# Interleaved quarters: the two transfers of each expert-weight tile take alternate pieces of the rows

## The chip, the cores and the metric

The kernel runs on one core of a Trainium2 chip. The core has a matrix engine (TensorE, PE in the profile, with its weight loads as PEld), a vector engine (VectorE, DVE), an activation engine (ScalarE, ACT), a general engine (GpSimd, POOL) and a small engine that here only issues transfers (SyncE, SP). Transfers are carried out by 16 DMA engines that all issuing engines share. Each engine works through its own list of instructions in order, and waits on semaphores where it needs the result of another engine or of a transfer.

The metric is the device time of one execution in microseconds (us), lower being better. The profile's clock covers the span from the first to the last instruction of the program; the time of the execution is a little longer.

## What is computed

Two blocks stand one after the other. The first is a linear attention with a delta rule, for 4 batches of 8 heads, 768 steps and a head size of 48:

```python
for t in range(S):
    kt, vt, bt = (k_n[:, :, t], v[:, :, t], beta[:, :, t, None])
    y[:, :, t] = np.einsum('bhd,bhde->bhe', q[:, :, t], state)
    v_old = np.einsum('bhde,bhd->bhe', state, kt)
    state = state + bt[:, :, :, None] * np.einsum('bhd,bhe->bhde', kt, vt - v_old)
```

`k_n` is `k` with each row scaled to length one. Its output, 3072 rows of 384 columns, goes into a mixture of 8 experts with 4 slots each. A softmax over the rows mixes them into 32 slots, each expert puts its 4 slots through two products, and a softmax over the slots mixes them back:

```python
logits = x @ phi
d = softmax over rows of logits;  c = softmax over slots of logits
slot_input = d.T @ x                      # 32 x 384
for e in range(E):                        # 8 experts, 4 slots each
    h = np.maximum(slot_input[e] @ w1[e], 0.0)   # w1[e]: 384 x 1024
    slot_out[e] = h @ w2[e]                      # w2[e]: 1024 x 384
return c @ slot_out
```

All inputs and the output are 32-bit floats. The weights `w1` and `w2` are 12.6 MB each (8 x 384 x 1024 x 4 bytes).

## The kernel before

**The sequence is cut into chunks.** The 768 steps are 12 chunks of 64. For a chunk, `load` (L399) brings `k` and `v`, and `load_q` (L416) `q`, in rows of 192 bytes; `prep` (L481) transposes them and multiplies keys with keys and queries. The recursion within a chunk becomes the inverse of a triangular matrix. `invert` (L550) works for two chunks at a time on blocks of 16, column by column, with small multiplications and subtractions (all issued through the helper `tt`, L277) that a table gives to DVE or to POOL. `join` (L641) puts blocks of 16 together into blocks of 64: `madd` (L702, also through L277) makes a sum that the products at L716 need. `step` (L803) then takes the chunks one after the other, since the state passes from each to the next; its products are at L782, L791, L821 and L840. `route` (L894) and `pair` (L910) gather the logits and the running softmax for the slots.

**The experts come last.** `first` (L1080) multiplies the slots with `w1` (L1090) for four experts at a time, in two halves of 512 columns; `qq` is the group of four. `prod` of the second stage (L1119, the product at L1123) multiplies with `w2`, in two passes `h` over 192 of the 384 output columns; each pass goes through all 32 tiles of `w2`. L1142 mixes the slots back to rows, L277's neighbours L281 and L283 copy results out of the accumulators, and L1150 writes the output.

**The weights are loaded long before.** A tile of `w1` is 128 partitions by 1024 columns (one of the 3 slices `kk` of an expert); there are 24. A tile of `w2` is 128 partitions by 768 columns (rows `2 tp` and `2 tp + 1` of each partition); there are 32. Each tile is brought by two transfers, issued one right after the other by the same engine, SP or POOL (the loops at L1021 and L1032). Tiles go into one memory in which each address is used many times over, so a transfer can start only when what stood there has been read.

**The order is fixed by hand.** Every piece of work is an `Op` with the engines that could do it. Three tables written into the file set everything: `ORDER` (L17) is the order of all pieces, and so the order on every engine; `ALTS` (L108) names the engine of each; `PLACE` (L75) its addresses. `Plan.run` (L186) issues the pieces in that order. The semaphores and waits are not written in the kernel: a layer below finds out which instructions touch the same memory and places them. A transfer adds to one of eight semaphores per kind of queue, taken in turn (one set for SP and ACT, one for POOL).

SP carries 32 transfers of `w1`, 46 of `w2` and most of `q`, `k` and `v`. POOL carries 16 of `w1`, 18 of `w2` and a few of the others, between its share of the arithmetic.

Of the kernel before, what the change touches and what calls it, by code (L numbers as in the profile page):

```python
# [196 lines left out]
def kernel(  # L197
# [17 lines left out]
    E, Dm, F = moe_w1.shape  # L215
# [14 lines left out]
    def A(b, n=None):  # L230
        if b.psum:
            return pb[:, b.addr:b.addr + b.size, :]
        return sb[:, b.addr:b.addr + (n or b.size)]
# [37 lines left out]
    def dq(a, b, c):  # L271
        return [("SP", a), ("POOL", b)] + ([("ACT", c)] if c else [])

    ENG = {"SP": nc.sync, "ACT": nc.scalar, "POOL": nc.gpsimd, "DVE": nc.vector}
# [104 lines left out]
    def perm():  # L379
        for x in H2:  # L380
# [3 lines left out]
          w=[(cmA, 1)])  # L384
# [14 lines left out]
    def load(src, n, pad):  # L399
        t = kslot[n % NK] if pad else pl.buf(KW)  # L400
        s = src.rearrange("b h s d -> s (b h) d")

        d = lambda: A(t).rearrange("p (x d) -> p x d", x=16)[:, :, 0:D]
        for r in H2:
            h0 = 16 * (1 - r)
            parts = [(64 * r, 64, slice(0, 16, 2), n * C, slice(h0, h0 + 16, 2))]
            for k in range(4):
                parts.append((64 * r + 16 * k, 16, slice(1, 16, 2), n * C + 48 - 16 * k, slice(h0 + 1, h0 + 16, 2)))

            def go(e, ps=parts):  # L410
                for p0, w, x, t0, hs in ps:
                    ENG[e].dma_start(out=d()[p0:p0 + w, x], in_=s[t0:t0 + w, hs])  # L412
            pl.op(dq(2.6, 2.95, 2.5 if src is k and n < 2 else None), None, go, w=[(t, 2 * r)], bus=1.5, nd=5)
        return t

    def load_q(n):  # L416
# [3 lines left out]
        for r in H2:  # L420
# [6 lines left out]
          w=[bnat], bus=0.1)  # L427
# [35 lines left out]
    def turn(src, n, a):  # L463
        if n not in KQ:
            KQ[n] = pl.buf(2048)
        dst = KQ[n]
        for h in H2:
            ps = pl.buf(1, psum=True)

            def go(h=h, ps=ps):  # L470
                for j in range(4):
                    x = P * (4 * h + j)
                    nc.tensor.transpose(A(ps)[:, 0, P * j:P * j + P], A(src)[:, x:x + P], ident())  # L473
            pl.op("PE", 0.53, go, r=[src, cident], w=[ps], rec=4, hold=[dst], act=512)

            def tev(e, h=h, ps=ps):
                copy(e, kqv(dst)[:, 4 * h:4 * h + 4, :, a],
                     A(ps)[:, 0].rearrange("p (j r t) -> p j r t", j=4, r=2))
            pl.op(ev(512), None, tev, r=[ps], w=[(dst, 2 * a + h)])
# [305 lines left out]
    def query(n):  # L785
        pY = late[n][0]

        def go():
            for j in range(8):
                for r in H2:  # L790
                    mm(A(pY)[ha(1 - r), j // 4, 96 * (j % 4):96 * (j % 4) + 96], kqv(KQ[n])[:, j, r, 1], Sv(n)[:, j, r],  # L791
                       start=j % 4 == 0)
        pl.op("PE", 1.47, go, r=[KQ[n], Sz[n % 2]], w=[pY], rec=32, act=1536)
# [227 lines left out]
    for e in range(E):  # L1021
        for kk in range(NKT):
            w1b[e, kk] = t = done.pop(0) if done else pl.buf(F)
            pl.tag = ("w1", e)

            def go(q, e=e, kk=kk, t=t):
                s = moe_w1[e].rearrange("(p k) f -> p k f", k=NKT)
                for x in H2:
                    ENG[q].dma_start(out=A(t)[:, 512 * x:512 * x + 512], in_=s[:, kk, 512 * x:512 * x + 512])
            pl.soft = [chain[8]]  # L1030
            pl.op(dq(0.8, 1.2, None), None, go, w=[t], bus=1.5, nd=2)
    for e in range(E):  # L1032
        for tp in range(NFC // 2):
            w2b[e, tp] = t = last.pop() if last and e == E - 1 else pl.buf(2 * Dm)
            pl.tag = ("w2", e)

            def go(q, e=e, tp=tp, t=t):
                s = moe_w2[e].rearrange("(p t) d -> p t d", t=NFC)
                for x in H2:
                    ENG[q].dma_start(out=A(t)[:, Dm * x:Dm * x + Dm], in_=s[:, 2 * tp + x])  # L1040
            pl.soft = [chain[N - 1]]
            pl.op(dq(0.8, 1.2, None), None, go, w=[t], bus=1.15, nd=2)
    pl.soft = []
# [138 lines left out]
```

## Time and profile before

| | us |
|---|---|
| three runs | 298.03, 295.66, 298.94; median 298.03 |
| the profiled execution | 296.42 |
| its span | 294.7 |
| PE busy in the span | 228.9 (78%) |
| DVE busy | 197.6 (67%) |
| ACT busy | 145.2 (49%) |
| POOL busy | 140.2 (48%) |
| granted PE clock, mean | 0.938 of full speed |

SP's transfers (queue q1) took 42.3% of what 16 DMA engines could do in the span, POOL's (q0) 15.0%.

How to read what is quoted. A row such as `187.01 3.30 POOL L1029 DMA_DIRECT2D sb<-in_moe_w_dram  x6 [2.04 <-ACT sb L513]` comes from the timeline: start and length in us, engine, line, operation, what it writes and reads, how many in a row, and in brackets the idle time of the engine before it and who ended it. `SPq` is the list of SP, where an issue stands with the time that it took SP to issue it, not with the transfer's own. `sb` is the on-chip memory, `pb` the accumulators, `in_moe_w_dram` the weights `w1` or `w2`: the line tells which. A row `POOLq DMA_DIRECT2D x16, 256.0 KB, 5.3` of the DMA view gives the number of issues, the size of each and the median time in us from issue to landing. A row of a line's own view (`L1040 SPq ... x46: 327/335/1575`) gives the shortest, median and longest duration in ns.

### The profile page before, as it was taken

The numbers are of one execution on the slowest core, as the hardware profiler recorded it, in microseconds if no ns is written. First come the engines' busy times: TensorE is split into PE (matmuls) and PEld (weight loads), VectorE is DVE, ScalarE is ACT, GpSimd is POOL, SyncE is SP. The second block draws the span as 40 slices with busy tenths as digits, with TensorE's granted clock in tenths as the row PEclk, the third lists the DMA queues.
The fourth block names the chain that finished last, engine by engine and source line by source line (L and its number), as shares of the span: only waits on it lengthen the run. The fifth ranks groups of instructions, "written<-read, shape, count | busy, mean of one in ns | idle before, by whom it ended". The sixth has DMA issues, their size and how long they took to land.

```text
span 294.7 us, 14440 instructions
## 1 busy us (share of the span) xinstructions
PE 228.9 (78%) x6252; PEld 186.2 (63%) x6252; DVE 197.6 (67%) x504; ACT 145.2 (49%) x325; POOL 140.2 (48%) x225
## 2 busy tenths in 40 slices
PE   0784778982988897798979877787866988999950
PEld 0663677872887786686868775766654864366640
DVE  3468979989866689777699889883773667213130
ACT  1253487774828466668736768562311532230321
POOL 8997569454493364226762545641640320200460
PEclk9997599999579999999899999999997999999985
DMA  8979642453431361336545407785696599990887
GB/s 147 162 155 166 111 79 56 97 107 56 87 56 34 73 118 33 62 54 136 116 94 118 153 4 232 215 190 177 200 349 218 178 349 375 349 364 13 213 226 206
DMA packets 81519, 45.13 MB, mean 153 GB/s; under 512 B 63520, under 2 KB 74704, under 8 KB 81456
## 3 DMA queue, kind: packets, MB, share of 16 engines
q1 hardware_dynamic: 72704, 30.28, 42.3%
q0 software_dynamic: 5232, 12.56, 15.0%
q10 hardware_dynamic: 3520, 1.38, 2.0%
q8 instruction: 49, 0.80, 1.1%
q14 instruction: 14, 0.11, 0.1%
HBM read 39.47 MB, written 4.72 MB: 150 GB/s over the span
## 4 chain that ended last, share of the span: by engine, by line
PE 27%; DVE 12%; issue 8%; SPq 4%; ACT 4%; POOL 2%; DMA 1%; DVEq 0%; POOLq 0%; ACTq 0%
SPq L1150 4%; DVE sb L277 4%; PE pb L1090 4%; PE pb L716 3%; PE pb L821 3%; ACT sb L281 2%; PE pb L1123 2%; PE pb L782 2%; PE pb L902 2%; PE pb L791 2%; POOL sb L277 2%; PE pb L504 2%; PE pb L867 1%; PE pb L920 1%; PE pb L953 1%
## 5 line engine op out<-in xcount | busy, mean ns | idle before, releaser
L281 ACT ACTIVATE sb<-pb 128x512 f32<-128x512 f32 (+5 forms) x144 | 76.0, 559 | 91.2 <-PE pb L473 22.9
L277 POOL TENSOR_TENSOR sb<-sb 128x256 f32<-128x256 f32 (+10 forms) x89 | 64.7, 735 | 66.8 <-DVE sb L277 33.5
L277 DVE TENSOR_TENSOR sb<-sb 128x126 f32<-128x126 f32 (+10 forms) x153 | 52.9, 347 | 11.2 <-POOL sb L277 6.7
L283 DVE COPY sb<-pb 128x512 f32<-128x512 f32 (+5 forms) x43 | 26.2, 617 | 27.3 <-PE pb L473 5.9
L473 PE MATMUL pb<-sb 128*128 128x128 f32 x192 | 32.7, 318 | 15.0 <-DMA sb<-in_q_dram 9.6
L473 PEld LDWEIGHTS pb<-sb 128*128 128x128 f32 x192 | 24.7, 161 | 19.4 <-issue 11.7
L716 PE MATMUL pb<-sb 64*64 64x32 f32 x1152 | 27.3, 231 | 11.9 <-DVE sb L277 4.7
L716 PEld LDWEIGHTS pb<-sb 64*64 64x64 f32 x1152 | 25.0, 147 | 15.2 <-issue 7.3
L504 PE MATMUL pb<-sb 64*64 64x128 f32 x768 | 28.2, 287 | 5.8 <-ACT sb L281 4.2
L840 PE MATMUL pb<-sb 64*64 64x48 f32 x768 | 26.2, 220 | 3.9 <-DVE sb L770 1.9
L840 PEld LDWEIGHTS pb<-sb 64*64 64x64 f32 x768 | 24.2, 135 | 6.6 <-DVE sb L770 2.5
L504 PEld LDWEIGHTS pb<-sb 64*64 64x64 f32 x768 | 22.7, 140 | 9.0 <-ACT sb L281 5.4
L782 PE MATMUL pb<-sb 64*64 64x48 f32 x768 | 26.0, 220 | 2.3 <-issue 2.3
L782 PEld LDWEIGHTS pb<-sb 64*64 64x64 f32 x768 | 24.1, 135 | 2.7 <-issue 2.5
L1040 POOL DMA_DIRECT2D sb<-in_moe_w_dram x18 | 9.7, 543 | 32.9 <-PE pb L953 16.1
L821 PE MATMUL pb<-sb 128*64 128x96 f32 x352 | 19.2, 260 | 3.2 <-ACT sb L281 1.6
L791 PE MATMUL pb<-sb 128*64 128x96 f32 x352 | 18.9, 261 | 1.9 <-ACT sb L513 0.8
L412 POOL DMA_DIRECT2D sb<-in_k_dram x35 | 19.7, 570 | 0.7 <-DVE sb L341 0.7
L821 PEld LDWEIGHTS pb<-sb 128*64 128x64 f32 x352 | 16.8, 145 | 4.9 <-ACT sb L281 2.2
L1150 POOL DMA_DIRECT2D out_dram<-sb x14 | 8.4, 607 | 23.8 <-DVE sb L283 18.5
L513 ACT ACTIVATE sb<-pb,sb 128x128 f32<-128x128 f32 x48 | 16.9, 368 | 4.9 <-PE pb L504 4.7
L791 PEld LDWEIGHTS pb<-sb 128*64 128x64 f32 x352 | 16.4, 145 | 3.6 <-issue 1.5
(142 smaller groups left out, 376.4 us busy)
## 6 DMA issues: line engine op xcount, KB each, us to landing
sb<-in_moe_w_dram SPq DMA_DIRECT2D x46, 192.0 KB, 5.5
sb<-in_moe_w_dram SPq DMA_DIRECT2D x32, 256.0 KB, 4.0
sb<-in_moe_w_dram POOLq DMA_DIRECT2D x16, 256.0 KB, 5.3
sb<-in_moe_w_dram POOLq DMA_DIRECT2D x18, 192.0 KB, 6.1
sb<-in_q_dram SPq DMA_DIRECT2D x14, 192.0 KB, 4.4
out_dram<-sb SPq DMA_DIRECT2D x24, 96.0 KB, 3.5
sb<-in_v_dram SPq DMA_DIRECT2D x22, 96.0 KB, 3.3
sb<-in_v_dram SPq DMA_DIRECT2D x88, 24.0 KB, 2.8
```

The lines of the kernel that those rows point to most:

```text
L277: ENG[e].tensor_tensor(*a, **kw)
L281: nc.scalar.activation(o, i, ACT.Copy)
L283: V.tensor_copy(o, i)
L412: ENG[e].dma_start(out=d()[p0:p0 + w, x], in_=s[t0:t0 + w, hs])
L473: nc.tensor.transpose(A(ps)[:, 0, P * j:P * j + P], A(src)[:, x:x + P], ident())
L504: mm(A(ps)[ha(r), c, P * j4:P * j4 + P].rearrange("p (a t) -> p a t", a=2), x[ha(c), j, r, 0], x[ha(c), j, r])
L716: mm(A(ps)[ha(b), x, 64 * j:64 * j + RW].rearrange("p (a t) -> p a t", t=w), st, m)
L782: mm(pv(pY)[ha(1 - r), j // 4, j % 4, c], A(at)[ha(r), 512 * c + 64 * j:512 * c + 64 * j + 64], hv(u)[ha(r), j, c], start=first and c == 0 ...
L791: mm(A(pY)[ha(1 - r), j // 4, 96 * (j % 4):96 * (j % 4) + 96], kqv(KQ[n])[:, j, r, 1], Sv(n)[:, j, r], start=j % 4 == 0)
L821: mm(A(pR)[ha(r), j // 4, 96 * (j % 4):96 * (j % 4) + 96], kqv(KQ[n])[:, j, r, 0], Sv(n)[:, j, r])
L840: mm(pv(pW)[ha(r), j // 4, j % 4, c], A(zs)[ha(r), 64 * (zj * c + z0 + j):64 * (zj * c + z0 + j) + 64], hv(R)[ha(r), j, c])
L1150: ENG[e].dma_start(out=o[y, b, z][:, 2 * g2:2 * g2 + 2, HD * h:HD * h + HD], in_=A(ob)[ha(y), Dm * b:Dm * b + Dm].rearrange("p (x d) -> p ...
```

## The change

Both transfers of a tile stay, on the same engine and in the same place of the order. What each brings is changed. Before, the first brought the left half of the tile's columns and the second the right half, so that each partition's share was one run (2 KB of `w1`, 1.5 KB of `w2`). After, the columns are taken as four quarters, and the first transfer brings quarters 0 and 2, the second quarters 1 and 3, so that each partition's share is two runs (of 1 KB or 768 bytes). For `w2` the quarters are the two halves of the output columns for each of its two rows.

```diff
@@ w1 @@
                 for x in H2:
-                    ENG[q].dma_start(out=A(t)[:, 512 * x:512 * x + 512], in_=s[:, kk, 512 * x:512 * x + 512])
+                    part = lambda w: w.rearrange("p (a b f) -> p a b f", a=2, b=2)[:, :, x]
+                    ENG[q].dma_start(out=part(A(t)), in_=part(s[:, kk]))
@@ w2 @@
                 for x in H2:
-                    ENG[q].dma_start(out=A(t)[:, Dm * x:Dm * x + Dm], in_=s[:, 2 * tp + x])
+                    ENG[q].dma_start(out=A(t, 2 * Dm).rearrange("p (t b f) -> p t b f", t=2, b=2)[:, :, x],
+                                     in_=s[:, 2 * tp:2 * tp + 2].rearrange("p t (b f) -> p t b f", b=2)[:, :, x])
```

Lines after L1029 move down by one, and after the second place by two: `w1` is issued at L1030 and `w2` at L1041 in the profile after, the products are at L1092 and L1125, and the output is written at L1152.

## The prediction

> **What bounds the kernel now.** I read the page first, for the span and the chain of waits that ended last.
>
> ```profile
> span 294.7 us, 14440 instructions
> PE 27%; DVE 12%; issue 8%; SPq 4%; ACT 4%; POOL 2%; DMA 1%; DVEq 0%; POOLq 0%; ACTq 0%
> ```
>
> The end is set by a chain of small steps that passes from TensorE (PE) to VectorE (DVE), ScalarE (ACT) and GpSimd (POOL); transfers have 1% of it. So the weights cost almost nothing today. Whether that holds under the change is a question of how close they are to that chain. The stretches before the end tell:
>
> ```profile
> 240.00:250.00 10.00, 7.88 (x89) 4.55 (x85) 6.35 (x28) 4.36 (x17) 1.07 (x2) 1.00 1.05 382
> 250.00:260.00 10.00, 10.00 (x96) 2.84 (x88) 2.02 (x10) 2.15 (x4) 2.12 (x4) 1.00 1.01 355
> ...
> 249.64 10.51 PE L1090 MATMUL pb<-sb 128*32 128x512 f32 x96 [0.15 <-DVE sb L1069]
> 262.54 6.06 PE L1123 MATMUL pb<-sb 128*32 128x192 f32 x144
> ```
>
> The last three columns of the first two rows are PE clock, DMA share and GB/s: the 16 DMA engines are full (1.05 and 1.01) while PE multiplies with the weights (L1090 the first product, L1123 the second) without a gap. The weights come just in time, by little. The queue that issues most of them is SyncE's (SP); its timeline from 204 us on, start and length of each run of issues:
>
> ```profile
> 204.46 1.23 SPq L1029 DMA_DIRECT2D sb<-in_moe_w_dram  x2
> ...
> 205.74 2.81 SPq L412 DMA_DIRECT2D sb<-in_v_dram  x5
> 208.78 4.63 SPq L1029 DMA_DIRECT2D sb<-in_moe_w_dram  x8
> 213.46 12.91 SPq L1040 DMA_DIRECT2D sb<-in_moe_w_dram  x6
> 226.46 0.86 SPq L1029 DMA_DIRECT2D sb<-in_moe_w_dram  x2
> 228.45 10.60 SPq L1040 DMA_DIRECT2D sb<-in_moe_w_dram  x12
> 239.90 0.81 SPq L1029 DMA_DIRECT2D sb<-in_moe_w_dram  x2
> 241.39 7.97 SPq L1040 DMA_DIRECT2D sb<-in_moe_w_dram  x10
> 249.53 1.12 SPq L1029 DMA_DIRECT2D sb<-in_moe_w_dram  x2
> 250.75 11.84 SPq L1040 DMA_DIRECT2D sb<-in_moe_w_dram  x18
> ```
>
> L1029 is w1, L1040 is w2, two issues to a tile: 8 pairs of w1, 46 issues of w2 and 5 of v.
>
> **The change, part by part.** The number of transfers, their order and their bytes stay. Three things change.
>
> *A wait inside each pair of w1 (the part that decides).* The built program's list of instructions, with the semaphores each waits for, shows it. A transfer adds to one of eight semaphores in turn (DMAHW0 to 7 on SP, DMASW0 to 7 on POOL), and waits for that one to be free. The same w1 pair before and after:
>
> ```
> before  DMACopy sb<-in_moe_w_dram 128x512 [waits DMAHW4_49,Pool_49]
>         DMACopy sb<-in_moe_w_dram 128x512 [waits DMAHW5_49]
> after   DMACopy sb<-in_moe_w_dram 128x2x256 [waits DMAHW4_49,Pool_49]
>         DMACopy sb<-in_moe_w_dram 128x2x256 [waits DMAHW5_49,DMAHW4_49]
> ```
>
> The second now also waits for DMAHW4, with the count that the first one reaches on landing. The quarters interleave, and the layer that places the waits takes the two transfers to write over each other. This stands at all 24 w1 pairs (16 on SP, 8 on POOL), at none of w2. An engine's queue is in order, so what stands behind the second half waits too: on POOL the elementwise work, on SP v and all later weights. What one wait costs is the landing time of a first half. The answers (POOL, one issue at 160.5 us; the page's medians of all w1 on POOL and on SP; SP in a quiet stretch, 198 to 206 us, its line and its landing times), then POOL's timeline:
>
> ```profile
> sb<-in_moe_w_dram POOLq DMA_DIRECT2D x1, 256.0 KB, 3.5
> ...
> sb<-in_moe_w_dram POOLq DMA_DIRECT2D x16, 256.0 KB, 5.3
> sb<-in_moe_w_dram SPq DMA_DIRECT2D x32, 256.0 KB, 4.0
> ...
> L1029 SPq DMA_DIRECT2D sb<-in_moe_w_dram x6: 327/337/431, 198.9 to 205.4; - x6
> DMA to landing us min/median/max: 2.6/2.8/3.2
> ...
> 160.53 1.16 POOL L1029 DMA_DIRECT2D sb<-in_moe_w_dram  x2
> 162.92 0.86 POOL L277 TENSOR_TENSOR sb<-sb 128x110 f32<-128x110 f32 x2 [1.24 <-DVE sb L277]
> 164.67 1.10 POOL L1029 DMA_DIRECT2D sb<-in_moe_w_dram  x2
> 165.78 1.29 POOL L277 TENSOR_TENSOR sb<-sb 128x512 f32<-128x512 f32 x1
> 168.97 0.84 POOL L277 TENSOR_TENSOR sb<-sb 128x256 f32<-128x256 f32 x1 [1.90 <-DVE sb L618]
> 177.53 1.10 POOL L1029 DMA_DIRECT2D sb<-in_moe_w_dram  x2
> 183.66 1.31 POOL L277 TENSOR_TENSOR sb<-sb 128x30 f32<-128x30 f32 x4 [3.52 <-DVE sb L277]
> 187.01 3.30 POOL L1029 DMA_DIRECT2D sb<-in_moe_w_dram  x6 [2.04 <-ACT sb L513]
> 190.31 2.30 POOL L412 DMA_DIRECT2D sb<-in_v_dram  x4
> 195.53 0.84 POOL L277 TENSOR_TENSOR sb<-sb 128x256 f32<-128x256 f32 x1 [1.61 <-DVE sb L626]
> ```
>
> First step, POOL at 160 us. The second half starts at 160.53 + 3.5 = 164.03 and ends 0.55 later (1.16 or 1.10 for two), at 164.58; the L277 at 162.92 is 1.66 late. The pair at 164.67 becomes 166.33; its second half starts 3.8 later (just above the 3.5: POOL and SP now both load) and ends at 170.68; the 128x512 after it takes 1.29, to 171.97. The L277 at 168.97 starts then: 3.0 late. PE waits for just that one (1.4 us at L716 already, the first row below), and the join behind it is on the chain. Term: **+3.0**.
>
> ```profile
> PEld pb L716 <- POOL sb L277: 1.4, 1, 1.4
> ...
> 197.78 0.70 PE pb L716 x37
> ```
>
> The pair at 177.53 holds POOL 3.75 - 0.55 = 3.2 longer, and 3.52 of idle time stands before the next L277: hidden, barely; cover gone, it costs what it exceeds.
>
> Second step, POOL at 187 us: three pairs in a row. Each takes a landing and an issue, 3.75 + 0.54 = 4.29, together 12.87 in place of 3.30: 9.57 later, with the v transfers behind. I take 3.75 for the landing: near the single 3.5, and not the median 5.3, for pairs that wait hold fewer bytes in flight. The L277 at 195.53 had 1.61 of idle time, and PE takes its result at 197.78 although it ends at 196.37, another 1.4. Term: 9.57 - 1.61 - 1.4 = **+6.6**. PE's chain is then 9.6 late. The two POOL pairs at 234 us stand before weights that have some 10 us more by then: nothing.
>
> Third step, SP. Its 16 pairs wait too. Those before 204 us delay v and k, which are issued far ahead; I cost them at nothing, and if they are not, each costs up to a landing. From the pair at 204.46, which waits for PE and so starts at 214.1, I add up the queue. What one issue of the new form costs, no row of w1 or w2 shows; near it are these (128 partitions by three runs; the old w2 form; 64 by two), and SP's own spacing:
>
> ```profile
> L456 SPq DMA_DIRECT2D sb<-in_moe_phi_dram x1: 432/432/432, 12.0 to 12.0; - x1
> ...
> L1040 SPq DMA_DIRECT2D sb<-in_moe_w_dram x46: 327/335/1575, 213.5 to 262.3; - x46
> ...
> L1150 SPq DMA_DIRECT2D out_dram<-sb x24: 595/626/1495, 271.8 to 291.3; - x24
> ...
> 253.63 1.85 SPq L1040 DMA_DIRECT2D sb<-in_moe_w_dram  x4
> ```
>
> I take 432 ns, the row with the same 128 partitions: 0.10 more than 327. Ends: 0 and 0.27 more (595). Four clean issues in 1.85 us, the last 0.43 long, are 0.47 apart; with the waits of a full queue 11.84 / 18 = 0.66. The middle, 0.57, and 0.10 make 0.67. A pair costs its landing and 0.6. Six pairs in light traffic: 6 x (2.8 + 0.6) = 20.4. Two behind a full queue (5.3): 2 x 5.9 = 11.8. 46 w2: 30.8. 5 v: 208.78 - 205.74 = 3.0. Sum 66.0, to 280.1. The last tile's first half starts two issues earlier, 278.8, and lands 4.1 later (row below), at **282.9**. Before, PE began the last tile in the last eighth of 128 of the 144 products: 262.54 + 6.06 x 112/144 = 267.3, and the span ended 27.4 after. So 282.9 + 27.4 = 310.3, which is 15.6 over 294.7 and takes in the 9.6.
>
> *POOL's issues.* 34 with twice the runs; 0.54 before, and 0.60 for the output form (L1150). 34 x 0.06 = 2 us, spread over 120 us and lying beside the waits above: nothing.
>
> *The packets.* Twice as many, half as long. Windows of the DMA view, q1 = SP's queue, packets, MB and share of 16 engines: w2 alone (256.5 to 263 us, with its landing), then 192 B rows (40 to 60 us).
>
> ```profile
> q1 hardware_dynamic: 1348, 1.84, 80.5%
> sb<-in_moe_w_dram SPq DMA_DIRECT2D x9, 192.0 KB, 4.1
> ...
> q1 hardware_dynamic: 4500, 0.82, 22.2%
> ```
>
> 80.5% of 16 x 6.5 us over 1348 packets is 62 ns (1,365 B in the mean); 22.2% of 16 x 20 over 4500 is 15.8 ns (182 B). The line between: 9 ns and 0.039 a byte. Two packets of 768 B cost 78 ns where one of 1,536 cost 69, 13% more. If the engines stayed the bound from 238 to 266 us, that is 13% of some 24 us of w2: 3 us, less a slack under 1: +2.5. But in the sum above SP issues a w2 half every 0.67 us, 293 GB/s, under the 355 the engines did: hidden. Should SP keep its pace, it is back.
>
> The Trainium skill, "DMA: Bandwidth & Descriptors", Specifications, gives 512 B as the smallest transfer at line rate. By it this term would be nil even where the engines bind, and 296.4 would stay; the two q1 rows do not agree.
>
> *Where a gain could lie.* In the list after, the first pass of w2 (output columns 0 to 191) waits for first halves alone, the second pass for second halves. That is up to one issue, 0.6, at the end; it is in the 278.8.
>
> The sum: 294.7 + 15.6 = 310.3 of span, and 1.7 around it (the profiled execution took 296.42) make **312**. The median of the runs shown is 298.03, 0.5% above the profiled execution; I leave the sum at the latter.
>
> **Rivals.**
> - Only POOL's waits count; SP makes up its own in the time in which it waited for PE. Speaks for it: PE waits from 204 on are part of SP's 58 us. Against: 66 us of work are more than that. 296.4 + 9.6 = 306. Chance 0.13.
> - The waits cost what busy stretches show: 4.0 on SP and 5.3 for POOL's triple (the medians above), 0.27 more an issue. POOL: 3.0 + 3 x 5.84 - 3.30 - 3.0 = 14.2; SP: 218.7 + 6 x 4.8 + 2 x 6.1 + 46 x 0.84 + 3.0 = 301.3, last landing 303.7, end 331.1. 333. Against: fewer bytes in flight. Chance 0.12.
> - Light landings everywhere, 2.6 for all. POOL: 0.9 + 3 x 3.14 - 3.30 - 3.0 = +4.0; SP: 208.5 + 8 x 3.2 + 33.8 = 267.9, landing 270.7, end 298.1, under the 298.7 of POOL. 300.4. Chance 0.05. The skill's same page, "Anatomy of one DMA", has 2.0 us and bytes / 436 GB/s, which gives 2.6 for 256 KB; the trace agrees with SP's least, not with POOL's 3.5.
> - Packets alone: all waits lie in idle time, w2 is 2.5 late: 299. Chance 0.04.
> - Not slower: POOL's and SP's waits are hidden and the first pass, needing only first halves, takes up the packets. It decides if a first half lands within the idle time behind it, 1.24 at 162.92; the landings quoted are 2.6 and more. 296.4. Chance 0.06.
>
> **How the numbers follow.** The forecast, 312, has 0.60. The range 301 to 329 leaves out the last two rivals and the upper half of the heavy one, about 0.16; above, it stops short of 333 because all three prices would have to be high at once. Faster by over 1%: 0.02, from the last rival; within 1%: 0.05, the rest of it and part of the packets; slower: 0.93. (1% is about what a measurement of this kernel can tell from no change.)
>
> **What would show it.** POOL's two L1029 at 160 us stand 3.5 us apart in place of 0.6, and the six at 187 take 11 to 14 us. PE is 2 to 4 late at 175 us and 8 to 11 at 205. SP's L1029 pairs have a wait for a weight transfer between them, and PE gets idle time for weights inside L1090 and L1123. The DMA share at the end falls under 0.95. Wrong if the second halves go out at once, if POOL's triple is made up by later idle time, or if the DMA share stays at 1.0 there, which would point to the packets.

## The result, and the profile after

The changed kernel takes 328.83 us (median of 4 runs, 325.89 to 330.0), the kernel before 297.45 us (median of 4, 295.66 to 298.94). The ratio is 1.1043, with a 95% interval of 1.0942 to 1.1143: about 31 us slower, where 15.6 had been forecast. Some executions of every kernel here fall into a slower state; medians are over all runs of a kernel, ratios and their intervals over the other runs alone. The execution that was profiled took 330.0 us. The page's span, and its chain of waits by engine:

```profile
span 328.3 us, 14460 instructions
PE 28%; DMA 11%; DVE 8%; issue 7%; POOL 4%; ACT 3%; SPq 0%; DVEq 0%; POOLq 0%
```

Transfers (DMA) have 11% of the chain where they had 1%, some 36 us of 328. The list of waits tells who stands and what comes last (total us, times, longest); the first three rows are those of the engines, the last that of SP's queue:

```profile
PE pb L1092 <- DMA sb<-in_moe_w_dram: 16.7, 2, 10.1
PEld pb L716 <- POOL sb L277: 14.0, 4, 6.9
POOL sb L1030 <- DMA sb<-in_moe_w_dram: 13.4, 4, 4.1
...
SPq L1030 <- DMA sb<-in_moe_w_dram: 57.7, 18, 7.9
```

The queues stand at w1 (L1030) until a weight transfer has landed: SP for 57.7 us. In the kernel before, the same wait of SP's queue was 2.9 us, in 3 times. PE stands in the first product (L1092) for 16.7 us, where it did not stand before. Its timeline, to be read beside the prediction's rows for L1090 and L1123:

```profile
259.53 2.84 PE L1092 MATMUL pb<-sb 128*32 128x512 f32 x20 [0.15 <-DVE sb L1071]
272.47 7.65 PE L1092 MATMUL pb<-sb 128*32 128x512 f32 x50 [10.09 <-DMA sb<-in_moe_w_dram]
286.69 6.49 PE L1092 MATMUL pb<-sb 128*32 128x512 f32 x26 [6.57 <-DMA sb<-in_moe_w_dram]
...
295.51 6.06 PE L1125 MATMUL pb<-sb 128*32 128x192 f32 x144
```

Two distances can be read here. The first product begins 9.9 us late (259.53 against 249.64): that is the chain, delayed by POOL. The second begins 33.0 us late (295.51 against 262.54): the other 23 us arise within the first product, which waits for two w1 tiles. The waits are 16.7 us of them (10.09 + 6.57); the other 6.5 are slower multiplications (2.84 + 7.65 + 6.49 us in place of 10.51). SP's queue in that time, and its last two issues:

```profile
219.55 3.87 SPq L1030 DMA_DIRECT2D sb<-in_moe_w_dram  x3
223.47 2.82 SPq L412 DMA_DIRECT2D sb<-in_v_dram  x5
226.52 18.98 SPq L1030 DMA_DIRECT2D sb<-in_moe_w_dram  x8
245.55 3.77 SPq L1041 DMA_DIRECT2D sb<-in_moe_w_dram  x6
249.37 5.68 SPq L1030 DMA_DIRECT2D sb<-in_moe_w_dram  x2
255.15 8.23 SPq L1041 DMA_DIRECT2D sb<-in_moe_w_dram  x12
263.90 6.01 SPq L1030 DMA_DIRECT2D sb<-in_moe_w_dram  x2
270.25 4.98 SPq L1041 DMA_DIRECT2D sb<-in_moe_w_dram  x10
275.40 8.77 SPq L1030 DMA_DIRECT2D sb<-in_moe_w_dram  x2
284.28 10.08 SPq L1041 DMA_DIRECT2D sb<-in_moe_w_dram  x18
...
293.44 0.92 SPq L1041 DMA_DIRECT2D sb<-in_moe_w_dram  x2
```

A run of w1 holds the queue for several times what the same run held it before: eight issues 18.98 us in place of 4.63, the last pair 8.77 in place of 1.12. The tile of the pair at 263.90 ends PE's first wait, that of the pair at 275.40 its second. The windows of the end, with PE clock, DMA share and GB/s as their last three columns, show what this does to both engines:

```profile
260.00:265.00 5.00, 2.37 (x20) 0.99 (x12) 1.03 (x5) 0.00 (x0) 0.00 (x0) 1.00 1.05 327
265.00:270.00 5.00, 0.00 (x0) 0.00 (x0) 0.00 (x0) 0.00 (x0) 0.00 (x0) 0.52 0.65 197
270.00:275.00 5.00, 2.53 (x13) 1.04 (x17) 0.00 (x0) 0.00 (x0) 0.18 (x1) 0.50 0.81 219
275.00:280.00 5.00, 5.00 (x42) 1.92 (x34) 0.70 (x4) 1.46 (x3) 2.71 (x4) 0.95 1.06 342
280.00:285.00 5.00, 0.12 (x1) 0.00 (x0) 0.21 (x1) 0.00 (x0) 0.00 (x0) 0.73 0.34 103
285.00:290.00 5.00, 3.31 (x16) 0.90 (x20) 0.00 (x0) 0.69 (x1) 0.00 (x0) 0.50 0.89 261
```

The DMA engines, which were full in the kernel before while PE multiplied with `w1`, fall to a share of 0.34 (280 to 285 us) while PE has nothing to multiply: the weights are late, and little is being fetched. PE's granted clock falls to 0.50. Last, POOL's timeline at the two places where the prediction costed it:

```profile
161.82 0.76 POOL L1030 DMA_DIRECT2D sb<-in_moe_w_dram  x1
166.09 0.72 POOL L1030 DMA_DIRECT2D sb<-in_moe_w_dram  x1 [3.51 <-DMA sb<-in_moe_w_dram]
...
194.11 0.75 POOL L1030 DMA_DIRECT2D sb<-in_moe_w_dram  x1 [0.26 <-ACT sb L513]
198.95 1.44 POOL L1030 DMA_DIRECT2D sb<-in_moe_w_dram  x2 [4.08 <-DMA sb<-in_moe_w_dram]
...
208.37 0.72 POOL L1030 DMA_DIRECT2D sb<-in_moe_w_dram  x1 [3.62 <-issue]
```

The two halves of one pair stand 4.27 us apart (161.82 to 166.09) and 0.60 before; the three pairs in a row take 15.0 us (194.11 to 209.09) and 3.30 before.

### The profile page after: what moved, and what is told of

The parts are those of the page before. It is cut to its first block, busy times and chain, and to the rows that moved or that the text cites. A ratio compares the mean times of both kernels' runs of the same rounds, so it can differ in the third digit from the quotient of the medians.

```text
span 328.3 us, 14460 instructions
## 1 busy us (share of the span) xinstructions
PE 239.8 (73%) x6252; PEld 193.9 (59%) x6252; DVE 196.7 (60%) x504; ACT 145.1 (44%) x325; POOL 145.9 (44%) x225
## 3 DMA queue, kind: packets, MB, share of 16 engines
q0 software_dynamic: 5232, 12.56, 14.5%
## 4 chain that ended last, share of the span: by engine, by line
PE 28%; DMA 11%; DVE 8%; issue 7%; POOL 4%; ACT 3%; SPq 0%; DVEq 0%; POOLq 0%
DMA sb<-in_moe_w_dram 10%; PE pb L1125 3%; PE pb L791 3%; PE pb L716 3%; PE pb L821 2%; POOL sb L277 2%; PE pb L1144 2%; PE pb L1092 2%; ACT sb L281 2%; PE pb L902 2%; PE pb L504 2%; PE pb L473 2%; PE pb L867 1%; PE pb L782 1%; DVE sb L277 1%
## 5 line engine op out<-in xcount | busy, mean ns | idle before, releaser
L277 POOL TENSOR_TENSOR sb<-sb 128x256 f32<-128x256 f32 (+10 forms) x89 | 64.3, 731 | 62.3 <-DVE sb L277 31.9
L277 DVE TENSOR_TENSOR sb<-sb 128x126 f32<-128x126 f32 (+10 forms) x153 | 51.7, 339 | 12.4 <-POOL sb L277 8.0
L716 PE MATMUL pb<-sb 64*64 64x32 f32 x1152 | 28.7, 240 | 20.9 <-POOL sb L277 13.2
L716 PEld LDWEIGHTS pb<-sb 64*64 64x64 f32 x1152 | 26.6, 158 | 24.4 <-POOL sb L277 14.0
L1092 PE MATMUL pb<-sb 128*32 128x512 f32 x96 | 17.0, 779 | 16.8 <-DMA sb<-in_moe_w_dram 16.7
L840 PEld LDWEIGHTS pb<-sb 64*64 64x64 f32 x768 | 24.6, 139 | 6.1 <-DVE sb L770 1.9
L504 PEld LDWEIGHTS pb<-sb 64*64 64x64 f32 x768 | 22.7, 140 | 9.3 <-ACT sb L281 5.4
L1041 POOL DMA_DIRECT2D sb<-in_moe_w_dram x18 | 13.0, 725 | 29.4 <-PE pb L1092 17.0
L1030 POOL DMA_DIRECT2D sb<-in_moe_w_dram x16 | 11.7, 729 | 30.7 <-DMA sb<-in_moe_w_dram 13.4
L782 PEld LDWEIGHTS pb<-sb 64*64 64x64 f32 x768 | 24.6, 138 | 0.1
L791 PE MATMUL pb<-sb 128*64 128x96 f32 x352 | 21.4, 283 | 3.3 <-DVE sb L827 1.9
L1152 POOL DMA_DIRECT2D out_dram<-sb x14 | 8.4, 606 | 34.5 <-DVE sb L283 28.2
L791 PEld LDWEIGHTS pb<-sb 128*64 128x64 f32 x352 | 18.8, 162 | 5.1 <-DVE sb L827 2.0
L1092 PEld LDWEIGHTS pb<-sb 128*32 128x32 f32 x96 | 5.8, 135 | 26.9 <-issue 26.3
```

The costliest lines, as they stand in the source:

```text
L277: ENG[e].tensor_tensor(*a, **kw)
L504: mm(A(ps)[ha(r), c, P * j4:P * j4 + P].rearrange("p (a t) -> p a t", a=2), x[ha(c), j, r, 0], x[ha(c), j, r])
L716: mm(A(ps)[ha(b), x, 64 * j:64 * j + RW].rearrange("p (a t) -> p a t", t=w), st, m)
L782: mm(pv(pY)[ha(1 - r), j // 4, j % 4, c], A(at)[ha(r), 512 * c + 64 * j:512 * c + 64 * j + 64], hv(u)[ha(r), j, c], start=first and c == 0 ...
L840: mm(pv(pW)[ha(r), j // 4, j % 4, c], A(zs)[ha(r), 64 * (zj * c + z0 + j):64 * (zj * c + z0 + j) + 64], hv(R)[ha(r), j, c])
L1041: ENG[q].dma_start(out=A(t, 2 * Dm).rearrange("p (t b f) -> p t b f", t=2, b=2)[:, :, x], in_=s[:, 2 * tp:2 * tp + 2].rearrange("p t (b f) ...
```

## The experiments

The theory: the waits inside the w1 pairs, on SP and on POOL, cost the time. The rival: smaller packets, and the issues that need more of them, cost it. Four kernels separate the two, five then divide the waits by queue and place, one looks at the clock, one goes the other way. Each ratio is to the kernel before, on the same chip; "over" is that ratio less 1, of some 298.4 us.

**One half of the change at a time.** w1 as in the change with w2 as before, then the reverse (the code in short form).

```diff
  w1_alone: w1 as changed;  w2: out=A(t)[:, Dm * x:Dm * x + Dm], in_=s[:, 2 * tp + x]
  w2_alone: w2 as changed;  w1: out=A(t)[:, 512 * x:512 * x + 512], in_=s[:, kk, 512 * x:512 * x + 512]
```

> Only the w1 edit: 24 pairs in quarters, each with its wait; w2 in whole rows as before. If the waits inside the pairs cost the time, nearly all of it is here: 28 to 33 us over before. If smaller packets cost it, about half of it, since w1 and w2 bring about equal bytes (6.3 and 4.7 MB): 12 to 20 us over before.

> Only the w2 edit: small packets and dearer issues of all w2, but no wait is added; w1 as before. If the waits cost the time: within 1% of before (0 to +3 us). If smaller packets cost it: 10 to 15 us over before.

The expectation's 6.3 and 4.7 MB are wrong: w1 and w2 bring 12.6 MB each. With w1 alone: 326.23 us, ratio 1.1042 (1.0933 to 1.1150), the whole loss. With w2 alone: 301.29 us, ratio 1.0156 (1.0075 to 1.0237), 4.7 over: more than the 1% that the theory gave it, though the interval reaches below 1%, and far from the rival's 10 us. Its small price can be seen in the second product, PE's timeline of the kernel with w2 alone:

```profile
250.31 10.51 PE L1091 MATMUL pb<-sb 128*32 128x512 f32 x96 [0.15 <-DVE sb L1070]
263.21 1.18 PE L1124 MATMUL pb<-sb 128*32 128x192 f32 x22
265.18 0.86 PE L1124 MATMUL pb<-sb 128*32 128x192 f32 x16 [0.80 <-DMA sb<-in_moe_w_dram]
266.39 0.85 PE L1124 MATMUL pb<-sb 128*32 128x192 f32 x14 [0.35 <-DMA sb<-in_moe_w_dram]
268.77 5.77 PE L1124 MATMUL pb<-sb 128*32 128x192 f32 x92 [1.53 <-DMA sb<-in_moe_w_dram]
```

The first product runs as before; the second, 6.06 us without a gap before, takes from 263.21 to 274.54, 5.3 longer. Of this, 2.7 are waits for w2, which arrives more slowly than PE takes it; the rest is slower multiplication behind the waits, where the granted clock was 0.50 (270 to 272 us).

**Small packets without the wait.** The quarters are read from memory as in the change, but each half lands in a contiguous half of the tile, so that the two transfers of a pair do not interleave where they write. The first product then yields its columns in another order, and the relu puts them back.

```diff
-                    ENG[q].dma_start(out=part(A(t)), in_=part(s[:, kk]))
+                    ENG[q].dma_start(out=A(t)[:, 512 * x:512 * x + 512].rearrange("p (a f) -> p a f", a=2),
+                                     in_=part(s[:, kk]))
...
-                o = A(hr)[:, f * HF:f * HF + HF]
+                o = A(hr).rearrange("p (a b f) -> p a b f", a=2, b=2)[:, :, f]
...      (the input of the relu is viewed likewise)
```

> Packets and issues of the changed kernel, w1 and w2, but each first half of w1 is laid down in its own contiguous half of the tile (the relu puts the columns back), so that no second half waits for its first. If the waits cost the time: within 1.5% of before (0 to +4 us), and what is left is the price of the packets and of the dearer issues. If smaller packets cost it: about as slow as the changed kernel, 28 to 33 us over before.

302.61 us, ratio 1.0185 (1.0095 to 1.0274), 5.5 over: a little above the theory's bound, and far from the rival's 28. What is left is put down to packets and issues; the relu with its reordered columns took 687 ns, as before. SP's queue row of the DMA view from 245 to 260 us (packets, MB, share of 16 engines), first of the kernel before, then of this one:

```profile
q1 hardware_dynamic: 2984, 4.25, 81.7%
```

```profile
q1 hardware_dynamic: 5743, 4.42, 96.5%
```

81.7% of 16 x 15 us over 4.25 MB is 46.1 us of engine time for a MB; 96.5% over 4.42 MB is 52.4, 14% more. The engines are full in both. The rate of all transfers in this window fell by less than that, from 361 to 331 GB/s, 8%.

**The wait without small packets.** Contiguous halves as before, but the second begins 16 columns early and writes them a second time.

```diff
-                    ENG[q].dma_start(out=A(t)[:, 512 * x:512 * x + 512], in_=s[:, kk, 512 * x:512 * x + 512])
+                    lo = 496 * x
+                    ENG[q].dma_start(out=A(t)[:, lo:512 * x + 512], in_=s[:, kk, lo:512 * x + 512])
```

> Contiguous halves and long packets as before, but the second half of each w1 pair begins 16 columns early and writes them again, with the same values (3% more bytes in that half), so that it waits for its first. If the waits cost the time: 25 to 33 us over before. If smaller packets cost it: 0 to 2 us over before.

325.49 us, ratio 1.0954 (1.0838 to 1.1071): packets as long as before, and nearly the whole loss. SP's queue waits as in the changed kernel:

```profile
SPq L1030 <- DMA sb<-in_moe_w_dram: 57.1, 18, 6.6
```

The four together settle the first question: the wait costs, with or without small packets; the packets do not cost much without the wait.

**The waits of one queue at a time.** In the form of the change are only the pairs of POOL, then only those of SP; the others and w2 are as before. Here and in the next cut the line that defines `part` is left out.

```diff
+                    if q == "POOL":      # second kernel: "SP"
+                        ENG[q].dma_start(out=part(A(t)), in_=part(s[:, kk]))
+                    else:
                         ENG[q].dma_start(out=A(t)[:, 512 * x:512 * x + 512], in_=s[:, kk, 512 * x:512 * x + 512])
```

> Only the 8 w1 pairs that POOL issues are in quarters and have the wait; SP's 16 pairs and all of w2 as before. If the chain's delay by POOL (12 us by 198 us in the changed kernel) lasts to the end and adds to SP's part: 7 to 12 us over before. If POOL's delay is only shadow, made up by 250 us or hidden beside late weights: 0 to 4 us.

> Only the 16 w1 pairs that SP issues are in quarters and have the wait; POOL's pairs and w2 as before. If the two parts add: 15 to 22 us over before. If SP's queue sets the end alone, whatever the chain does: 24 to 31 us over before. If SP makes up its waits in the time in which it waited for PE: 0 to 5 us.

POOL's pairs: 310.79 us, ratio 1.0414 (1.0345 to 1.0483), 12.4 over. SP's pairs: 317.59 us, ratio 1.0637 (1.0570 to 1.0705), 19.0 over. The sum, 31.4, is the loss of the whole within the intervals (some 2 us each): the parts add. Why they do is in PE's timelines, of POOL's pairs and then of SP's:

```profile
263.85 10.61 PE L1094 MATMUL pb<-sb 128*32 128x512 f32 x96 [0.15 <-DVE sb L1073]
```

```profile
246.98 1.90 PE L1094 MATMUL pb<-sb 128*32 128x512 f32 x10 [0.15 <-DVE sb L1073]
252.44 3.54 PE L1094 MATMUL pb<-sb 128*32 128x512 f32 x10 [3.56 <-DMA sb<-in_moe_w_dram]
262.52 7.91 PE L1094 MATMUL pb<-sb 128*32 128x512 f32 x50 [6.54 <-DMA sb<-in_moe_w_dram]
275.45 5.70 PE L1094 MATMUL pb<-sb 128*32 128x512 f32 x26 [5.02 <-DMA sb<-in_moe_w_dram]
```

With POOL's pairs the chain reaches the first product 14.2 late (263.85 against 249.64) and then finds its weights there: 10.61 us without a gap. With SP's the chain is in time (246.98), and waits for weights three times. And SP's queue itself has to wait for PE at about 204 us, so that a chain delayed by POOL starts SP's queue later too: its run of eight w1 issues starts at 217.31 with SP's pairs alone and at 226.52 in the changed kernel, and its last pair at 265.56 and 275.40. The queue cannot hide its waits in the delay.

**Where SP loses it.** Of SP's 16 pairs only the last two, then only the first eight (all before 204 us), then only the six between have the form of the change, chosen by tile.

```diff
+                    if (e, kk) in ((6, 2), (3, 2)):      # the last two; or the first eight, or the six between
```

> Only the last two w1 pairs of SP, which the changed kernel issued at 263.90 and 275.40 with 5.6 and 8.4 us from the first to the second half, are in quarters and have the wait; all else as before. If the loss of SP's part arises here, behind the full queue: 6 to 14 us over before. If the six pairs before them carry it: 0 to 4 us.

> Only the first eight w1 pairs of SP, all ahead of 204 us, are in quarters and have the wait; all else as before. The prediction cost them at nothing: within 1% of before (0 to +2 us). If the v and k that stand behind them come late: each costs up to its landing of some 3 us, and 5 to 12 us are added.

> Only the six w1 pairs of SP from 204 to 240 us are in quarters and have the wait; the last two and all else as before. With 19 us for all sixteen and 7 for the last two: if the parts add in one queue, 9 to 13 us over before. If SP's queue makes up the middle waits while it waits for PE: 0 to 4 us, and the last two cost more in company than alone.

The last two: 306.21 us, ratio 1.0230 (1.0149 to 1.0312), 6.9 over. The first eight: 297.53 us, ratio 0.9959 (0.9919 to 1.0000): nothing. The six between: 306.23 us, ratio 1.0262 (1.0169 to 1.0356), 7.8 over, between the two expectations. Together that is some 15 of the 19.0. The other 4 are no more than the intervals together leave open; whether they appear only when all wait in one queue is not shown. The middle pairs are partly made up, as the SP timeline of that kernel shows beside the prediction's rows:

```profile
211.70 19.53 SPq L1031 DMA_DIRECT2D sb<-in_moe_w_dram  x8
...
259.91 10.94 SPq L1044 DMA_DIRECT2D sb<-in_moe_w_dram  x18
```

Eight issues take 14.9 us more than before (19.53 against 4.63), and the run starts 2.9 later, yet the last run of w2 starts only 9.2 later (259.91 against 250.75): between, the queue had time to make up.

**Keeping TensorE at work.** The clock of 0.50 in the changed kernel could be a price of its own. Here 40 multiplies that repeat the first weights' products stand ahead of the first half of each first product.

```diff
             def prod(f=f, ph=ph):
+                for i in range(0 if f else 40):
+                    j = i % 4
+                    mm(A(ph)[32 * j:32 * j + 32, 0], A(slb)[:, 0:NSL], A(w1b[4 * qq + j, 0])[:, 0:HF], start=True)
                 for kk in range(NKT):
```

> The changed kernel, with 40 multiplies that do nothing new (the first weights' products over again) ahead of the first half of each group's first product, so that TensorE works while the late w1 halves are under way (some 8.8 us each, at 10.5 us for 48). If its clock falls because it idled: granted clock near 1 in the stretch after the second wait, its last 26 records in 3 us in place of 6.5, and 2 to 5 us less than the changed kernel. If the low clock has another cause, or the weights set the end anyway: the same time as the changed kernel or more, and the stretch as long as there.

> The changed kernel itself, on the chip of this group, for comparison with the run that keeps TensorE busy: 1.09 to 1.11 times before.

328.74 us, ratio 1.1034 (1.0962 to 1.1106); the changed kernel beside it 329.26 us, ratio 1.0977 (1.0877 to 1.1077). No difference in time that can be measured, though the clock did what was expected. Windows and PE's timeline of the kernel that is kept busy (L1092 are the added multiplies, L1095 those of the product):

```profile
280.00:285.00 5.00, 5.00 (x52) 2.79 (x48) 0.23 (x1) 0.00 (x0) 0.00 (x0) 1.00 0.52 162
285.00:290.00 5.00, 5.00 (x52) 2.80 (x46) 0.00 (x0) 0.69 (x1) 0.00 (x0) 1.00 0.96 298
```

```profile
285.64 5.72 PE L1095 MATMUL pb<-sb 128*32 128x512 f32 x46
```

The clock is 1.00 in place of 0.73 and 0.50, and 46 records take 5.72 us, 0.12 each, where the 26 after the second wait took 6.49, 0.25 each. So the low clock came from idling. That it brought so little has two reasons. The added multiplies stand ahead of products that PE could do before the wait ended, so that 46 records remain at 285.64 where 26 would do; the second product starts at 293.69, 1.8 us earlier. And little could be won: the last w2 tile's first half is issued at 293.44 in the changed kernel and lands after 4.7 us (row below), at 298.1. PE needs it in the last eighth of the first pass, at 295.51 + 6.06 x 112/144 = 300.2. A faster PE could win no more than these 2.1 us before it had to wait for that tile (an estimate from the changed kernel's rows).

```profile
sb<-in_moe_w_dram SPq DMA_DIRECT2D x2, 192.0 KB, 4.7
```

**The other direction.** Each weight tile is one transfer with runs of 4 KB or 3 KB.

```diff
-                for x in H2:
-                    ENG[q].dma_start(out=A(t)[:, 512 * x:512 * x + 512], in_=s[:, kk, 512 * x:512 * x + 512])
+                ENG[q].dma_start(out=A(t), in_=s[:, kk])
...      (w2 likewise)
```

> The other direction: each weight tile as one transfer of whole 4 KB and 3 KB runs, half as many issues and packets, no wait inside a tile. By the line of packet times (8 ns and 0.037 a byte, from 36 and 84 ns) the full engines at the end save 5 to 6% of some 24 us: 1 to 2 us under before, if packets set the end there. If the larger transfers land later for the multiply that waits, or the packets are cut again: 0 to 4 us over before.

297.51 us, ratio 0.9976 (0.9931 to 1.0021): no difference that can be measured, though the interval does not rule out the 1 to 2 us. In the kernel before, the chain of waits had DMA at 1%; that half as many issues and packets bring nothing agrees with it. No version that beats the kernel before came out of these runs.

## Why the prediction fell short

The direction and the mechanism were right; the size was half. Two terms of the sum were too small: the landing of a first half in SP's queue, which is the larger, and POOL's first step, which made the chain and with it the start of SP's queue late.

- *The wait inside each w1 pair.* Right. It is in SP's and POOL's rows, and with w1 alone the whole loss is there.
- *POOL, first step (+3.0).* Too small. PE's own wait for L277 at L716 from 160 to 180 us grew as forecast, from 1.4 to 4.9 us, but the chain fell further behind: the first pair of rows below is one instruction of POOL before and after, 7.5 late. The first two pairs held POOL for 5.0 and 5.3 us (161.82 to 166.81, 168.58 to 173.87) where 4.05 and 4.35 were taken, by a longer landing and by issues of 0.72 in place of 0.55. That is 1.9 of the missing 4.5; 1.3 is a later start (161.82 against 160.53), which may be chance, since POOL's pairs alone started at 160.31 and were still 6.4 late here. The rest is open.
- *POOL, second step (+6.6).* Near. The products at L716 that began at 197.78 before begin at 212.79 (the third row), 15.0 late: 7.5 more than at the row before, which takes in the pair at 177.53. The triple takes 15.0 us where 12.87 were taken; more idle time than counted took that up.

```profile
176.31 1.28 POOL L277 TENSOR_TENSOR sb<-sb 128x512 f32<-128x512 f32 x1 [1.60 <-DVE sb L741]
183.84 1.28 POOL L277 TENSOR_TENSOR sb<-sb 128x512 f32<-128x512 f32 x1 [4.97 <-DVE sb L741]
...
212.79 2.03 PE pb L716 x63
```

PE's waits at L716 in the changed kernel, from 160 to 180 us and from 196 to 215:

```profile
PEld pb L716 <- POOL sb L277: 4.9, 1, 4.9
```

```profile
PEld pb L716 <- POOL sb L277: 6.9, 1, 6.9
```

- *POOL together.* At L716 the chain is 15.0 late, not 9.6. That the first product then begins 9.9 late, near the 9.6, is luck: some 5 us were made up on the way there, and why is open. With POOL's pairs alone the chain was 13.8 late at L716 and 14.2 at the first product, and the time 12.4 over (10.3 to 14.4 by the interval).
- *SP's pairs before 204 us: nothing.* Right by themselves (first eight alone: 0.9959). Behind the late chain the last of them cost 1.1, as said next.
- *SP's queue from 204 us: this step failed, by its prices.* The forecast had the last tile's first half land at 282.9; it landed at 298.1, 15.2 later, in three parts:
  - The start, 6.0. v was to be issued after one pair, at 214.1 + 3.4 = 217.5, and was at 223.47. The pair ahead of that one waits for PE's products at L716 and started 14.5 late (216.73 against 202.25), not 9.6; its own wait then held the queue for 3.3 us in place of 2.2.
  - The queue between, 8.7: 278.8 - 217.5 = 61.3 forecast, 293.44 - 223.47 = 70.0 measured. In this, by the rows of SP's timeline, each run counted to the start of the next, seven pairs were to take 5 x 3.4 + 2 x 5.9 = 28.8 and took 19.03 + 5.78 + 6.35 + 8.88 = 40.0, 11.2 more. The 44 issues of w2 to the last tile were to take 29.5 (0.67 each) and took 3.82 + 8.75 + 5.15 + 9.16 = 26.9 (0.61), 2.6 less.
  - The landing of the last tile's first half: 4.7 in place of 4.1, 0.6.

  So the term that was most mis-sized is the landing of a first half of w1. From a first half's issue to its second's, the five pairs that had been put in light traffic took 22.5 us in place of 14.0, and the two behind a full queue 14.1 in place of 10.6. The 2.8 us of the forecast came from a quiet stretch; but a pair stands behind what its queue and POOL's have in flight. The last one landed after 8.4 us (its issue's own row, below); in these 8.4 us the engines moved 2.07 MB, of which this half is 0.26.

```profile
DMA to landing us min/median/max: 8.4/8.4/8.4
```

- *"Pairs that wait hold fewer bytes in flight"*, by which the low landings were taken, holds only where nothing else is in flight. Of the four pairs in a row from 226.52, the first two waited 5.4 and 5.1 us, while w2 halves that POOL issued from 225 to 231 us were landing (until 236.1), and the next two 3.0 and 3.6. Between the last pairs stand 12 and 10 issues of w2 that hardly wait, and the DMA share is at 1.05 and 1.06 again (260 to 265 and 275 to 280 us).
- *The end (282.9 + 27.4).* Its form was right: the landing of the last tile at 298.1, 2.1 of slack, and 28.1 from the point of need make 328.3. What the step did not have is that PE stands earlier, in the first product, for w1 tiles that it needs before, and then multiplies at half clock. Both lie within the time to the last tile, but for the 2.1.
- *POOL's issues (0.60 in place of 0.54).* Too low: 0.72, see below. Most of the sum still lies beside waits, but the four issues of the first step stood in the chain's way.
- *Packets (+13%, hidden; 2.5 if not).* The 13% was right as a price in engine time (14% measured), and so was "hidden", to within the intervals of some 3 us: with the waits, small packets of w2 add nothing that can be measured (1.1042 without them, 1.1043 with). Without the waits SP keeps its pace and the term is back, as the text said, but at 4.7 us (w2 alone) to 5.5 us (both) in place of 2.5, SP's and POOL's dearer issues and the lower clock behind PE's waits included. By the rule of the Trainium skill quoted in the prediction ("DMA: Bandwidth & Descriptors", Specifications) runs of 768 B would be at line rate; the 52.4 us for a MB against 46.1 do not agree.
- *The rivals.* "Only POOL's waits" is out, since SP's pairs alone cost 19.0. "Heavy" (333) was nearest in time; its price for the pairs (5 x 4.8 + 2 x 6.1 = 36.2 for the seven) was nearer to 40.0, while its 0.84 for a w2 issue was not; its 14.2 for POOL was near the 15.0, but made up of 3.0 and 11.2 where 7.5 and 7.5 were measured. "Light landings" (300.4, which lay just outside the stated range as well) and "packets alone" are out. "Not slower" is out: no first half landed within 1.24 us.

## What to carry to other kernels

Before interleaving the destinations of two transfers, look in the built program's waits whether they now count as writing over each other: a wait inside a pair on an in-order queue holds up everything behind it, and it shows in the profile as a queue that waits for its own transfers while the DMA share falls. Cost such a wait by the landing time at its own place, behind all that is in flight there, not by a transfer in a quiet stretch. Delays on two queues can add, as here, when the one queue has to wait for the chain that the other delays.

## What the runs showed of the hardware

- After idling, TensorE's granted clock was 0.50 to 0.52 over whole windows of 5 us, and a record of the first product took 0.25 us in place of 0.11 (10.51 / 96 before). With work in the wait it was 1.00, and after 2.5 us of multiplications behind the first wait it was 0.95 again (275 to 280 us). The Trainium skill, "TensorE: Matmul & The Clock Gate", Part 1, has a gate that halves the clock after an idle window and opens it after a busy one; the rows agree in the two levels and in both directions.
- An issue by GpSimd cost 0.18 us more when each partition's share was two runs. The page's rows of the costliest groups (busy us, mean ns of one), w2 on POOL, before and after:

```profile
L1040 POOL DMA_DIRECT2D sb<-in_moe_w_dram x18 | 9.7, 543 | 32.9 <-PE pb L953 16.1 <-PE pb L1090 11.1 <-DVE sb L283 4.3
```

```profile
L1041 POOL DMA_DIRECT2D sb<-in_moe_w_dram x18 | 13.0, 725 | 29.4 <-PE pb L1092 17.0 <-PE pb L953 11.7 <-DVE sb L827 0.6
```

- The output's issue on POOL, 0.60, from which the forecast took its price, was no guide for this form.
